# Reordering the opening of a fused state-space and gated-FFN kernel: factors read from PSUM, an earlier cast, and a new order of loads, masks and filler matmuls

## The chip, the cores and the metric

The kernel runs on one core of one Trainium2 chip. The metric is the device time of one execution in microseconds (us); lower is better. A core has five engines that work side by side and wait for each other by semaphores: TensorE (PE in the profile, with its weight loads shown apart as PEld), VectorE (DVE), ScalarE (ACT), GpSimd (POOL) and SyncE (SP), which only starts transfers here.

## The reference, cut to what matters

Two stages follow each other. The first is a chunked scan for 4 batches of 8 heads, 768 tokens, head size 32 and state size 16. With `cum` the cumulative sum of `log a` in a chunk:

```python
M = einsum('bhin,bhjn->bhij', Cc, Bc) * exp(cum[i] - cum[j]) * causal
y = einsum('bhij,bhjd->bhid', M, xc) + einsum('bhin,bhnd->bhid', Cc, state) * exp(cum)
state = exp(sum(la)) * state + sum_j(Bc * xc * exp(cum[-1] - cum))
```

The second takes the 3,072 x 256 result as tokens of a gated feed-forward net with 1,536 hidden units:

```python
out = (maximum(x @ w_gate, 0) * (x @ w_val)) @ w_out
```

## The kernel before, in words

The kernel works in pairs of 128-token chunks (256 tokens, "pair p"; three pairs make a batch, twelve make the whole) and in blocks of 512 tokens for the feed-forward net. Decays are not taken through logarithms: a cumulative product of `a` is scanned, C is multiplied by it and B by its reciprocal, so that `exp(cum[i] - cum[j])` comes out of the product of the two.

A pair goes through these steps, each a helper. `load_bc` and `load_x` bring B, C and x. `scale_wide(p, j, eng)` (line 303) multiplies C (j = 1) or B (j = 0) by the factors in the tile `wfac` and writes bf16. `transp(p, k, apart)` (line 356) transposes the result on PE, and `tevac(p, beng, ceng)` (line 369) brings it from PSUM to SBUF: `BT` by one copy on `beng`, `CT` by a multiplication with a mask on `ceng` (two ScalarE instructions, or one VectorE instruction). `G_wide(p)` (line 411) multiplies CT by BT into four PSUM banks, g0 to g3. `gmask(p, q, eng, psum)` applies the causal mask to bank q, either from PSUM or from a bf16 copy that `gcopy(p, q)` made on ScalarE before. `cast_x(p, eng)` makes x bf16, `adds(p)` forms the new state from B and x, `carry` and `pass_on` scale and hand the state on, `inter_wide(p)` adds the state's share and `D_wide(p, qs)` (line 515) the masked part of the result for the banks `qs`. `yevac_wide(p, A_, V)` evacuates the result of the pair to `yT`, one half on ScalarE, the other on VectorE.

The feed-forward net reads `yT`. `gvh(b, f, u, later)` (line 677) does one slice of 128 hidden units for half a block: four matmuls, then the ReLU on ScalarE at once, and a product on VectorE (`finish`), which `later=True` lets the caller place. Its own first lines show that the ReLU belongs to the call itself:

```python
        r = ffn.tile([128, 512], BF16, tag="r", name="r", bufs=5)[:, 0:256]
        nc.scalar.activation(r, gv_[:, 0], AF.Relu)
```

`factors()` gets the cumulative products of batch 0 into PSUM by matmuls. `scan(0, H)` scans all batches from `a_sb` on VectorE, and `decay()` (line 249) later turns that scan by fp32 matmuls into factors for the other batches, which `decay_factors()` copies to `scaleBC`. `weights(f0, f1)` starts transfers of the gate and value weights from GpSimd's queue. `keep_warm(n)` puts n matmuls on PE whose result nobody reads.

The order is written out by hand: lines 768 to 846 are the opening, one call after the other, and `in_order(tc)` (line 15) ties every engine to the order of the program, so that no instruction overtakes an earlier one on its engine. Across engines only the data and the buffers decide. PSUM tiles named by `bank` share five slots.

Of the kernel before, what the change touches and what calls it, by code (L numbers as in the profile page):

```python
# [29 lines left out]
def kernel(  # L30
# [46 lines left out]
    st = {}  # L77

    def load_bc(p, j, *qs):
        s = st.setdefault(p, {})  # L80
        if "bcr" not in s:
            s["bcr"] = raw.tile([128, NH, 2, 2, N], FP32, tag="bcr", name="bcr")
            if p == 2:
                nc.vector.memset(s["bcr"][0:1, 0, 1, 0, 0:1], 0.0)
        b, s0 = p // PPB, p % PPB * 256
        n = NH // len(qs)
        for i, q in enumerate(qs):
            hs = slice(i * n, (i + 1) * n)
            q.dma_start(
                out=s["bcr"][:, hs, j].rearrange("p h r n -> p h (r n)"),  # L90
                in_=(B, C)[j][b, hs, s0:s0 + 256, :].rearrange(
                    "h (p r) n -> p h (r n)", r=2))

    def load_x(p, *qs):
        xr = raw.tile([128, NH, 2, D], FP32, tag="xr", name="xr")
        if p == 2:
            nc.vector.memset(xr[0:1, 0, 0, 0:1], 0.0)
        b, s0 = p // PPB, p % PPB * 256
        n = NH // len(qs)
        for i, q in enumerate(qs):  # L100
            hs = slice(i * n, (i + 1) * n)
            q.dma_start(out=xr[:, hs].rearrange("p h r d -> p h (r d)"),
                        in_=x[b, hs, s0:s0 + 256, :].rearrange(
                            "h (p r) d -> p h (r d)", r=2))
        st.setdefault(p, {})["xr"] = xr
# [30 lines left out]
    nc.vector.memset(first, 0.0)  # L136
    load_bc(0, 1, nc.sync, nc.scalar)
    load_bc(0, 0, nc.sync, nc.scalar)
    a_sb = glob.tile([2 * BH, H], FP32)
    nc.sync.dma_start(out=a_sb, in_=a.rearrange("b h (w s) -> (b h w) s", w=2))  # L140
    load_x(0, nc.sync, nc.scalar)
    load_bc(1, 1, nc.sync)
    load_bc(1, 0, nc.scalar)
    load_x(1, nc.sync)
# [41 lines left out]
    def keep_warm(n, rhs=warm):  # L186
        w = bank("w", (128, 128))
        for _ in range(n):
            nc.tensor.matmul(out=w, lhsT=warm, rhs=rhs, start=True, stop=True)  # L189
# [5 lines left out]
    def weights(f0, f1, which=(0, 1)):  # L195
        fs = slice(f0 * 128, f1 * 128)
        for j in which:
            w, src = ((wg, moe_w_gate), (wv, moe_w_val))[j]
            nc.gpsimd.dma_start(  # L199
                out=w[:, :, fs], in_=src[:, fs].rearrange("(k p) f -> p k f", k=2))  # L200
# [12 lines left out]
    def factors():  # L213
        d = bank("fac", (128, 2, NH, PPB))
        for r in range(2):
            for i in range(2):
                nc.tensor.matmul(
                    out=d[64 * i:64 * i + 64, r].rearrange("p h k -> p (h k)"),
                    lhsT=cp0[:, r:128:2], rhs=idr[:, i:R:2], start=(r == 0), stop=True,
                    tile_position=(0, 64 * i), skip_group_check=True)  # L220
        return d
# [14 lines left out]
    def scan(s0, s1):  # L236
        nc.vector.tensor_tensor_scan(
            out=cp[:, s0:s1], data0=a_sb[:, s0:s1],
            data1=zero1.to_broadcast([2 * BH, s1 - s0]),
            initial=cp[:, s0 - 1:s0] if s0 else 1.0, op0=ALU.mult, op1=ALU.add)  # L240

    def middle():
        nc.vector.reciprocal(rmid, cp[:, H - 1:H])
        nc.vector.tensor_scalar_mul(pick[:, 0], pairs[:, 0], rmid)
# [3 lines left out]

    def decay():

        bank_ = mm.tile([128, HC * 2 * NB * 8 + 16], FP32, tag="tp", name="dec")
        n = HC * 2 * NB * 8
        d = bank_[:, 0:n].rearrange("p (k w b h) -> p k w b h", k=HC, w=2, b=NB)
        st["dec3"] = d3 = bank_[:, n:n + 16].rearrange("p (r h) -> p r h", r=2)
        for r in range(2):
            for i in range(2):
                nc.tensor.matmul(
                    out=d3[64 * i:64 * i + 64, r], lhsT=cp[:, i * 128 + r:i * 128 + 128:2],
                    rhs=pick[:, 0, NH:2 * NH], start=(r == 0), stop=True,
                    tile_position=(0, 64 * i), skip_group_check=True)  # L260
        for k in range(HC):
            nc.tensor.matmul(  # L262
                out=d[:, k].rearrange("p w b h -> p (w b h)"),
                lhsT=cp[:, k * 128:(k + 1) * 128],
                rhs=pick.rearrange("p w h -> p (w h)"),
                start=False, stop=True, skip_group_check=True)
        st["dec"] = d

    def decay_factors():
        d = st["dec"]  # L270
        nc.scalar.copy(out=fac3[:, 1], in_=st["dec3"])
        for w in range(2):
            cs = slice(w * HC, (w + 1) * HC)
            nc.scalar.copy(
                out=scaleBC[:, :, cs, 1, :].rearrange("p b k h -> p k b h"), in_=d[:, :, w])

    def inverse(b0, b1):
        for b in range(b0, b1):
# [24 lines left out]
    def scale_wide(p, j, eng):  # L303
        s = st[p]
        if p >= FIRST:
            s["bs"] = bs = tok[p % NTOK]
            src = s["bcr"].rearrange("s (t q) j r n -> s j r t q n", t=2)[:, j]
            for t in range(2):
                k = 2 * j * (1 + t)
                eng.tensor_tensor(  # L310
                    out=bs[:, k:k + 2].rearrange("s k (q t n) -> s k t q n", q=4, t=2)[:, :, t],
                    in0=src[:, :, t],
                    in1=fac3[:, j, :, 4 * t:4 * t + 4].to_broadcast([128, 2, 4, N]),
                    op=ALU.mult)
            return
        if "bs" not in s:
            s["bs"] = bs = att.tile([128, 4, 128], BF16, tag="bs", name="bs")
            s["tin"] = [[bs[:, 2 * j + r] for r in range(2)] for j in range(2)]
        src = s["bcr"].rearrange("s (t q) j r n -> s j r t q n", t=2)[:, j]
        f = wfac[:, j, :, :, p]  # L320
        for t in range(2):
            eng.tensor_tensor(  # L322
                out=s["bs"][:, 2 * j:2 * j + 2].rearrange(
                    "s k (q t n) -> s k t q n", q=4, t=2)[:, :, t],
                in0=src[:, :, t],
                in1=f[:, :, 4 * t:4 * t + 4].to_broadcast([128, 2, 4, N]),
                op=ALU.mult)
# [17 lines left out]
    def cast_x(p, ceng):  # L345
        s = st[p]
        cast = ceng.copy if ceng is nc.scalar else ceng.tensor_copy
        xb = att.tile([128, 2 * NH * D], BF16, tag="xb", name="xb")
        if p < NWIDE:
            cast(xb, s["xr"].rearrange("s h r d -> s (h r d)"))  # L350
            s["xb"] = xb.rearrange("s (h r d) -> s h r d", h=NH, r=2)
        else:
            cast(xb, s["xr"].rearrange("s i h d -> s (i h d)"))
            s["x"] = [xb[:, i * NH * D:(i + 1) * NH * D] for i in range(2)]
# [74 lines left out]
    def gmask(p, q, eng, psum=False):  # L429
        s = st[p]  # L430
        d = s["gw"][:, q]
        m = (wmask if p < FIRST else wmask3).unsqueeze(2).to_broadcast([128, 2, 2, 128])
        eng.tensor_tensor(out=d, in0=s["gp"][q] if psum else d, in1=m, op=ALU.mult)  # L433

    def gcopy(p, q):
        s = st[p]
        nc.scalar.copy(out=s["gw"][:, q], in_=s["gp"][q])
# [328 lines left out]
    V, A_, P_ = nc.vector, nc.scalar, nc.gpsimd  # L766

    keep_warm(22)
    d = factors()
    decays(0)  # L770
    keep_warm(8)
    nc.vector.tensor_copy(wfac[:, 1], d)
    nc.vector.memset(wg[0:1, 0, 0:1], 0.0)
    weights(0, 2)
    weights(2, 4)
    weights(4, 6, (0,))
    scale_wide(0, 1, V)
    nc.vector.reciprocal(wfac[:, 0, :, :, 0], wfac[:, 1, :, :, 0])
    scale_wide(0, 0, V)
    transp(0, 1, False)  # L780
    keep_warm(4)
    transp(0, 0, True)
    tevac(0, A_, V)
    nc.vector.reciprocal(wfac[:, 0, :, :, 1:3], wfac[:, 1, :, :, 1:3])
    scan(0, H)
    scale_wide(1, 1, P_)
    scale_wide(1, 0, P_)
    weights(4, 6, (1,))
    keep_warm(6)
    G_wide(0)  # L790
    keep_warm(7)
    gcopy(0, 0)
    gmask(0, 2, V, True)
    keep_warm(5, st[0]["gw"][:, 0, 0, 0])
    cast_x(0, A_)
    decays(1)
    adds(0)
    gmask(0, 3, V, True)
    keep_warm(4, st[0]["gw"][:, 3, 0, 0])
    gmask(0, 0, V)  # L800
    gmask(0, 1, V, True)
    pass_on(0, 0)
    carry(0, 0)
    middle()
    inter_wide(0)
    D_wide(0, (2, 3, 0))
    D_wide(0, (1,))
    turn(1, True)
    keep_warm(2)
    yevac_wide(0, A_, V)  # L810
    load_bc(2, 1, nc.sync)
# [3 lines left out]
    weights(8, NF)  # L815
    weights_out(0, NF // 2)
    weights_out(NF // 2, NF)
    tevac(1, V, A_)
    cast_x(1, V)
    pass_on(0, 1)  # L820
# [1 line left out]
        for f in fs:  # L822
            gvh(b, f, u)

    f0 = gvh(0, 0, 0, True)
    G_wide(1)
    decay()
    adds(1)
# [201 lines left out]
```

## Time and profile before

| What | Value |
|---|---|
| Time, median of 3 runs | 124.46 us (124.38 to 124.65) |
| Span of the profiled execution | 122.7 us |
| PE busy | 118.1 us (96%) |
| VectorE busy | 88.0 us (72%) |
| ScalarE busy | 76.3 us (62%) |
| GpSimd busy | 48.2 us (39%) |
| Granted TensorE clock | 1.0 of full |

The span of the profile is the one traced execution from its first to its last instruction; the time is measured around it and is a little longer. "Busy" is the share of the span in which an engine had at least one instruction running. The page also gives a row of busy tenths in forty slices, and the chain of waits that ended last. In the timeline of an engine each line has a start, a duration, the engine, the line of the kernel, the operation and the tiles that it writes and reads; where several of one kind follow each other they are merged with "x4" and the like. A bracket at the end gives the idle time before the instruction and what ended it.

### The profile page before, as it was taken

Reading aid. Unit: us, or ns where it says so; the run is one execution under the profiler, and the core shown is the slowest. Engines: PE = TensorE matmul, PEld = TensorE weight load, DVE = VectorE, ACT = ScalarE, POOL = GpSimd, SP = SyncE. Lnnn points to the kernel's source line nnn. Section 1 sums busy time; section 2 is a strip of 40 time slices with the busy share of each in tenths; the row PEclk is TensorE's granted clock in tenths of the full one; section 3 lists DMA queues with packets and bytes.
Section 4 is the critical chain, followed back from the end, with each engine's and each line's share of the span. In section 5 each row is a group of like instructions: output and inputs, shape, how many; then the busy total and the mean of one; then the engine's idle time right before and its main releaser. Section 6 shows DMA issues by size and latency. Waiting matters only on the chain.

```text
span 122.7 us, 3665 instructions
## 1 busy us (share of the span) xinstructions
PE 118.1 (96%) x1404; PEld 82.4 (67%) x1404; DVE 88.0 (72%) x200; ACT 76.3 (62%) x169; POOL 48.2 (39%) x108
## 2 busy tenths in 40 slices
PE   6989999999999999999999999999999999999990
PEld 6856784577875478874577864677854678844790
DVE  4798988872799864988763897855987656788410
ACT  0467688835987725786635886545877447876420
POOL 6499989361455127360351806033600033000000
DMA  3999999996979995999999498960580002200022
GB/s 63 220 208 146 171 192 194 189 172 103 115 89 139 143 142 143 103 150 205 150 114 140 154 136 138 110 117 0 189 52 0 0 0 91 85 0 0 0 91 86
DMA packets 77489, 13.93 MB, mean 113 GB/s; under 512 B 70064, under 2 KB 77472, under 8 KB 77472
## 3 DMA queue, kind: packets, MB, share of 16 engines
q1 hardware_dynamic: 70128, 10.61, 54.2%
q0 software_dynamic: 4288, 2.36, 14.1%
q10 hardware_dynamic: 3056, 0.72, 2.7%
q8 instruction: 11, 0.18, 0.6%
q14 instruction: 6, 0.05, 0.1%
HBM read 11.13 MB, written 3.15 MB: 116 GB/s over the span
## 4 chain that ended last, share of the span: by engine, by line
PE 92%; POOL 4%; DVE 1%; issue 1%; DVEq 0%
PE o L713 26%; PE gv L686 21%; PE gate L668 15%; PE val L671 15%; PE y L643 2%; PE g L548 2%; PE w L189 2%; POOL wg L199 2%; POOL bs L322 1%; PE y L632 1%; PE o L707 1%; PE A_ps L601 1%; PE g L418 1%; POOL wv L199 1%; PE y L523 1%; PE dec L262 1%
## 5 line engine op out<-in xcount | busy, mean ns | idle before, releaser
L675 DVE TENSOR_TENSOR h<-r,val 128x512 bf16<-128x512 bf16 x44 | 30.0, 685 | 7.3 <-ACT r L674 7.2
L713 PE MATMUL o<-wo,h 128*128 128x256 bf16 x276 | 33.1, 273 | 0.0
L674 ACT ACTIVATE r<-gate 128x512 bf16<-128x512 f32 x44 | 26.3, 597 | 9.7 <-PE gate L668 9.3
L713 PEld LDWEIGHTS <-h 128*128 128x128 bf16 x276 | 25.9, 98 | 5.3 <-issue 1.7
L668 PE MATMUL gate<-yT,wg 128*128 128x512 bf16 x88 | 26.2, 379 | 0.0
L671 PE MATMUL val<-yT,wv 128*128 128x512 bf16 x88 | 26.2, 379 | 0.0
L692 DVE TENSOR_TENSOR h<-r,gv 128x256 bf16<-128x256 bf16 x56 | 22.5, 419 | 2.6 <-ACT r L689 1.8
L689 ACT ACTIVATE r<-gv 128x256 bf16<-128x256 f32 x56 | 21.2, 386 | 2.3 <-PE gv L686 0.2
L686 PE MATMUL gv<-yT,wg 128*128 128x256 bf16 x112 | 21.5, 273 | 0.0
L686 PE MATMUL gv<-yT,wv 128*128 128x256 bf16 x112 | 21.4, 273 | 0.0
L556 POOL TENSOR_SCALAR_AFFINE_SELECT gs<-gs 128x512 bf16<-128x512 bf16 (+1 forms) x16 | 8.0, 523 | 30.0 <-ACT gs L567 30.0
L573 DVE TENSOR_TENSOR gs<-g,maskUT 128x512 bf16<-128x512 f32 x16 | 10.3, 685 | 11.4 <-issue 5.6
L338 POOL TENSOR_TENSOR tok<-bcr,scaleBC 128x128 bf16<-128x128 f32 x32 | 12.2, 409 | 14.1 <-DMA bcr<-in_B_dram 13.0
L671 PEld LDWEIGHTS <-wv 128*128 128x128 bf16 x88 | 8.6, 98 | 10.4
L668 PEld LDWEIGHTS <-wg 128*128 128x128 bf16 x88 | 8.6, 98 | 8.9
L686 PEld LDWEIGHTS <-wv 128*128 128x128 bf16 x112 | 11.0, 98 | 1.3
L686 PEld LDWEIGHTS <-wg 128*128 128x128 bf16 x112 | 10.2, 98 | 1.9 <-DVE yT L536 0.2
L567 ACT CAST gs<-g 128x512 bf16<-128x512 f32 x8 | 4.7, 589 | 6.7 <-PE g L548 6.7
L656 ACT CAST yT<-y 128x512 bf16<-128x512 f32 x8 | 4.7, 586 | 5.1 <-PE y L643 2.5
L433 DVE TENSOR_TENSOR gs<-g,wmask 128x512 bf16<-128x512 f32 x9 | 5.9, 680 | 2.6 <-PE g L418 2.6
L189 PE MATMUL w<-warm 128*128 128x128 bf16 x49 | 5.5, 284 | 1.1 <-DVE tmask L163 1.1
L189 PEld LDWEIGHTS <-warm 128*128 128x128 bf16 x58 | 5.0, 126 | 1.7 <-DVE tmask L163 1.1
(122 smaller groups left out, 115.8 us busy)
## 6 DMA issues: line engine op xcount, KB each, us to landing
xr<-in_x_dram SPq DMA_DIRECT2D x17, 128.0 KB, 3.2
out_dram<-ob SPq DMA_DIRECT2D x3, 512.0 KB, 3.2
bcr<-in_C_dram SPq DMA_DIRECT2D x17, 64.0 KB, 2.9
bcr<-in_B_dram SPq DMA_DIRECT2D x17, 64.0 KB, 2.9
out_dram<-ob SPq DMA_DIRECT2D x4, 256.0 KB, 3.5
xr<-in_x_dram SPq DMA_DIRECT2D x3, 256.0 KB, 4.1
wo<-in_moe_w_out_dram POOLq DMA_DIRECT2D x2, 384.0 KB, 8.5
wg<-in_moe_w_gate_dram POOLq DMA_DIRECT2D x4, 128.0 KB, 4.0
```

The costliest lines, as they stand in the source:

```text
L189: nc.tensor.matmul(out=w, lhsT=warm, rhs=rhs, start=True, stop=True)
L338: eng.tensor_tensor(out=dst[:, t, j * (1 + t)], in0=src[:, j, :, t], in1=f[:, j, :, 4 * t:4 * t + 4].to_broadcast([128, 2, 4, N]), op=ALU. ...
L556: nc.gpsimd.affine_select(out=dst, in_=dst, pattern=[[0, n], [1, 128]], compare_op=ALU.is_ge, fill=0.0, base=0, channel_multiplier=-1)
L573: nc.vector.tensor_tensor(out=d[:, q], in0=g[q], in1=m, op=ALU.mult)
L668: nc.tensor.matmul(out=g, lhsT=wg[:, k, fs], rhs=yT[:, k, tk], start=(k == 0), stop=(k == 1))
L671: nc.tensor.matmul(out=v, lhsT=wv[:, k, fs], rhs=yT[:, k, tk], start=(k == 0), stop=(k == 1))
L674: nc.scalar.activation(r, g, AF.Relu)
L675: nc.vector.tensor_tensor(out=fst[b][:, f], in0=r, in1=v, op=ALU.mult)
L686: nc.tensor.matmul(out=gv_[:, j], lhsT=w[:, k, fs], rhs=yT[:, k, tk], start=(k == 0), stop=(k == 1), skip_group_check=True)
L689: nc.scalar.activation(r, gv_[:, 0], AF.Relu)
L692: nc.vector.tensor_tensor(out=fst[b][:, f, u * 256:(u + 1) * 256], in0=r, in1=gv_[:, 1], op=ALU.mult)
L713: nc.tensor.matmul(out=o[:, ts % 2], lhsT=fst[b][:, f, ts * 128:(ts + 1) * 128], rhs=wo[:, f], start=(f == 0), stop=(f == NF - 1), skip_gr ...
```

## The change

All edits lie in the first 13 us, but for the shape of the matmuls in `decay()`. They aim at getting pair 0 through its steps sooner and at letting the weights and the first feed-forward slice come earlier.

1. x of pair 0 is loaded ahead of `a_sb` on SyncE's queue.
2. The factors of pair 0 are read where they lie: C is scaled by the PSUM tile `fac` itself, the reciprocal for B of pairs 0 and 1 is taken from it in one instruction, and the copy into `wfac` goes to ScalarE. The reciprocal for pair 2 moves behind `middle()`.
3. The six first weight transfers are started before anything is scaled; the sixth no longer waits behind GpSimd's scaling of pair 1.
4. x of pair 0 is cast before `G_wide(0)`, `adds(0)` comes before the masks, bank 1 also gets a ScalarE copy, and the masks go 2, 0, 1, 3, so `D_wide` leaves bank 3 for last. The counts of filler matmuls change.
5. The first feed-forward slice `f0` and `transp(1, 0)` now stand in front of `tevac(1)`, in that order; before, `f0` stood behind `tevac(1)`, `cast_x(1)` and `pass_on(0, 1)`.
6. `decay()` leaves out batch 0, whose factors nobody reads: 48 moving columns in place of 64.

```diff
-    a_sb = glob.tile([2 * BH, H], FP32)
-    nc.sync.dma_start(out=a_sb, in_=a.rearrange("b h (w s) -> (b h w) s", w=2))
     load_x(0, nc.sync, nc.scalar)
+    a_sb = glob.tile([2 * BH, H], FP32)
+    nc.sync.dma_start(out=a_sb, in_=a.rearrange("b h (w s) -> (b h w) s", w=2))
...
-                lhsT=cp[:, k * 128:(k + 1) * 128],
-                rhs=pick.rearrange("p w h -> p (w h)"),
+                lhsT=cp[:, k * 128:(k + 1) * 128], rhs=pick[:, :, NH:],
...
-        f = wfac[:, j, :, :, p]
+        f = fac[:, :, :, 0] if p == 0 and j else wfac[:, j, :, :, p]
...
     keep_warm(22)
-    d = factors()
+    fac = factors()
+    nc.vector.memset(wg[0:1, 0, 0:1], 0.0)
+    for f in (0, 2, 4):
+        weights(f, f + 2)
     decays(0)
-    keep_warm(8)
-    nc.vector.tensor_copy(wfac[:, 1], d)
-    nc.vector.memset(wg[0:1, 0, 0:1], 0.0)
-    weights(0, 2)
-    weights(2, 4)
-    weights(4, 6, (0,))
+    keep_warm(6)
     scale_wide(0, 1, V)
-    nc.vector.reciprocal(wfac[:, 0, :, :, 0], wfac[:, 1, :, :, 0])
+    nc.vector.reciprocal(wfac[:, 0, :, :, 0:2], fac[:, :, :, 0:2])
+    nc.scalar.copy(out=wfac[:, 1], in_=fac)
     scale_wide(0, 0, V)
...
     tevac(0, A_, V)
-    nc.vector.reciprocal(wfac[:, 0, :, :, 1:3], wfac[:, 1, :, :, 1:3])
     scan(0, H)
+    cast_x(0, A_)
     scale_wide(1, 1, P_)
     scale_wide(1, 0, P_)
-    weights(4, 6, (1,))
-    keep_warm(6)
+    keep_warm(4)
     G_wide(0)
     keep_warm(7)
+    adds(0)
     gcopy(0, 0)
     gmask(0, 2, V, True)
     keep_warm(5, st[0]["gw"][:, 0, 0, 0])
-    cast_x(0, A_)
+    gcopy(0, 1)
+    gmask(0, 0, V)
     decays(1)
-    adds(0)
+    keep_warm(4, st[0]["gw"][:, 2, 0, 0])
+    gmask(0, 1, V)
+    keep_warm(4, st[0]["gw"][:, 1, 0, 0])
     gmask(0, 3, V, True)
-    keep_warm(4, st[0]["gw"][:, 3, 0, 0])
-    gmask(0, 0, V)
-    gmask(0, 1, V, True)
     pass_on(0, 0)
     carry(0, 0)
     middle()
+    nc.vector.reciprocal(wfac[:, 0, :, :, 2], wfac[:, 1, :, :, 2])
     inter_wide(0)
-    D_wide(0, (2, 3, 0))
-    D_wide(0, (1,))
-    turn(1, True)
+    D_wide(0, (2, 0, 1))
+    D_wide(0, (3,))
+    transp(1, 1, True)
     keep_warm(2)
     yevac_wide(0, A_, V)
...
     weights_out(NF // 2, NF)
+    f0 = gvh(0, 0, 0, True)
+    transp(1, 0, True)
     tevac(1, V, A_)
     cast_x(1, V)
     pass_on(0, 1)
...
-    f0 = gvh(0, 0, 0, True)
     G_wide(1)
     decay()
```

More of the change, by code (lines that the diff above doesn't have):

```diff
@@ L138 @@
     load_bc(0, 0, nc.sync, nc.scalar)
+    load_x(0, nc.sync, nc.scalar)
     a_sb = glob.tile([2 * BH, H], FP32)
     nc.sync.dma_start(out=a_sb, in_=a.rearrange("b h (w s) -> (b h w) s", w=2))
-    load_x(0, nc.sync, nc.scalar)
     load_bc(1, 1, nc.sync)
@@ L249, in decay @@
     def decay():
[L251 to L254, printed above, removed]
+        n = HC * 2 * (NB - 1) * NH
+        bank_ = mm.tile([128, n + 2 * NH], FP32, tag="tp", name="dec")
+        d = bank_[:, 0:n].rearrange("p (k w b h) -> p k w b h", k=HC, w=2, b=NB - 1)
+        st["dec3"] = d3 = bank_[:, n:].rearrange("p (r h) -> p r h", r=2)
         for r in range(2):
@@ L262, in decay @@
             nc.tensor.matmul(
-                out=d[:, k].rearrange("p w b h -> p (w b h)"),
-                lhsT=cp[:, k * 128:(k + 1) * 128],
-                rhs=pick.rearrange("p w h -> p (w h)"),
+                out=d[:, k].rearrange("p w b h -> p w (b h)"),
+                lhsT=cp[:, k * 128:(k + 1) * 128], rhs=pick[:, :, NH:],
                 start=False, stop=True, skip_group_check=True)
@@ L274, in decay_factors @@
             nc.scalar.copy(
-                out=scaleBC[:, :, cs, 1, :].rearrange("p b k h -> p k b h"), in_=d[:, :, w])
+                out=scaleBC[:, 1:, cs, 1, :].rearrange("p b k h -> p k b h"), in_=d[:, :, w])
     def inverse(b0, b1):
```

## The prediction, made before the changed kernel was run

> **What bounds the kernel now.** I first read the page, then the engines' busy time from the first feed-forward matmul to the last one, then the chain of waits through the opening, then the timelines of ScalarE and VectorE there.
>
> ```profile
> span 122.7 us, 3665 instructions
> PE 118.1 (96%) x1404; PEld 82.4 (67%) x1404; DVE 88.0 (72%) x200; ACT 76.3 (62%) x169; POOL 48.2 (39%) x108
> ```
>
> ```profile
> 10.30:119.70 109.40, 109.40 (x1260) 75.58 (x1260) 79.89 (x168) 72.36 (x160) 40.55 (x88) 1.00 0.70 109
> ```
>
> The second line (stretch, its length, then busy PE, PEld, DVE, ACT, POOL) says that PE is never idle between 10.30 and 119.70 us. The end is therefore set by when PE's unbroken run begins and by how much work is in it. Only two things can move the time: a shift of that beginning, or work taken out of the run.
>
> ```profile
> 7.80 0.72 POOL wg L199
> 8.52 0.01 issue
> 8.54 1.70 POOL bs L322 x4
> 10.24 0.05 issue
> 10.28 0.28 PE tpb L367 x2
> 10.57 0.11 PE w L189 x2
> 10.68 0.45 PE gv L686 x4
> 11.13 0.39 PE g L418 x16
> 11.51 0.34 PE dec L257 x8
> 11.85 0.81 PE dec L262 x6
> ```
>
> This chain (start, us, what) is a near tie, not GpSimd's alone: the run begins with transp(1,0), which waited for GpSimd's scaling of pair 1, but f0's matmuls (gv) also need pair 0's result, and that is ready at 10.38, as the VectorE lines below show. The thing to see is what stands between f0 and G_wide(1): nothing. f0 fills PE for 0.45 us just while pair 1's transposes are evacuated.
>
> ```profile
> 9.92 0.37 ACT L540 CAST yT<-y 128x256 bf16<-128x256 f32 x1 [0.91 <-PE Aps L523]
> 10.19 0.84 ACT L385 ACTIVATE CT<-tp,tmask 128x256 bf16<-128x256 bf16 x2
> 10.92 0.35 ACT L486 ACTIVATE Sw<-T,dec 128x64 bf16<-128x64 f32 x1
> 11.16 0.38 ACT L689 ACTIVATE r<-gv 128x256 bf16<-128x256 f32 x1
> ```
>
> ```profile
> 6.39 0.89 DVE L237 TENSOR_TENSOR_SCAN cp<-a_sb,zero 64x384 f32<-64x384 f32 x1
> 7.21 1.25 DVE L433 TENSOR_TENSOR gs<-g,wmask 128x512 bf16<-128x512 f32 x2
> 8.38 0.47 DVE L433 TENSOR_TENSOR gs<-gs,wmask 128x512 bf16<-128x512 bf16 x1
> 8.78 0.68 DVE L433 TENSOR_TENSOR gs<-g,wmask 128x512 bf16<-128x512 f32 x1
> 9.38 0.14 DVE L243 RECIPROCAL rmid<-cp 64x1 f32<-64x1 f32 x1
> 9.56 0.34 DVE L244 TENSOR_SCALAR pick<-identf,rmid 64x32 f32<-64x32 f32 x1
> 9.96 0.42 DVE L540 CAST yT<-Aps 128x256 bf16<-128x256 f32 x1
> 10.61 0.29 DVE L392 COPY BT<-tpb 128x256 bf16<-128x256 bf16 x1
> ```
>
> On ScalarE the two CT multiplications of pair 1 stand ahead of f0's ReLU (r) and end at 11.03; G starts at 11.09. BT ended at 10.90. So G waits for CT, and CT follows the evacuation of pair 0 without a gap.
>
> **What the Trainium skill says.** "TensorE: Matmul & The Clock Gate", Part 1, says that ScalarE and VectorE take instructions strictly in order. The trace agrees: every timeline above follows the program, so an instruction that waits holds up all behind it. "DMA: Bandwidth & Descriptors", Queues, rings and completion order, says that descriptors of a ring are consumed in ring order and that a DMA engine takes turns between rings packet by packet. No run here shows the swap, but SyncE's `a_sb` (issued 2.29, 3.4 us to landing) does land before the x behind it (2.90, 3.9 us). "VectorE: DVE Perf Modes", The perf-mode tier table, gives a bf16 tensor_tensor from SBUF twice the rate of one from PSUM; here 128x512 take 0.41 to 0.47 us against 0.68 us. The TensorE page, Why this matters for your kernels, warns of idle gaps over some 3 us; the gap that I find below is under 1 us, and the gaps of this trace (clock 1.00) cost nothing visible.
>
> **Part by part: pair 0.** Scaling C from PSUM starts at 4.19 instead of 4.43: the copy's 0.24 us is gone from VectorE. The operand from PSUM isn't in the trace for this shape: at best the 0.286 us of one such scaling stays, at worst it grows by some 0.1 us; I take it unchanged, because the tier table named above has fp32 tensor_tensor at the single rate from either memory. The reciprocal over 32 columns costs 0.34 instead of 0.25, so 0.1 comes back. CT of pair 0 therefore starts at 5.38 instead of 5.53, and G(0) 0.15 earlier. The copy into wfac on ScalarE (0.2 us, from about 4.46, after its table load) lies beside VectorE's scaling. Six filler matmuls in place of eight end before C is scaled; they are no cost.
>
> The reciprocal at 6.13 (0.26 to the next start) leaves this place, so scan could start at 5.98. But `a_sb` is now behind half of x: issued at about 2.90, and its bytes moved to behind 512 short packets. In before the SyncE queue's packet count stands in `a_sb` from about 3.9 to 5.05 us, and the landing came 0.65 later. 512 short packets at the 150 per 0.25 us that this queue made beside ScalarE's take 0.85 us. So it lands between 6.0 (the rest goes faster) and 6.8 (the earlier weights compete); I take 6.45. Scan then starts at 6.45 and gains nothing; behind it on VectorE wait all four masks and the rest of pair 0, so the first mask starts at 7.27 (scan to mask was 0.82) instead of 7.21. ScalarE's cast of x (0.62) now stands at about 6.15, so its copies of g0 and g1 start near 6.74 and 7.22 and are done before VectorE needs them. The masks go at starts of 7.27, 7.84, 8.24 and 8.64 (0.57 behind a PSUM mask, 0.40 behind a bf16 one), and the last ends at 9.32 instead of 9.46: one mask became bf16 and saves 0.19. Bank 3's eight D matmuls then end at about 9.75. On VectorE middle() and the third reciprocal (0.25) come first: 9.24, 9.42, 9.72, evacuation 9.93 to 10.35. Before it was 9.96 to 10.38. Pair 0 thus gains only 0.03 us where the scan is late, and 0.25 where it isn't: f0 starts at 10.1 to 10.4, say 10.40.
>
> **Weights.** The flag (memset) moves from 4.34 to about 3.3, the first start from 4.73 to about 3.65. One start at 0.93 and five at 0.72 end at 8.2; the four scalings (1.70) end at 9.9 instead of 10.24. That removes the GpSimd wait from transp(1,0), but f0 at 10.40 is later, so it is worth nothing by itself. Weights for f0 land with a second to spare.
>
> **f0 ahead of transp(1,0) and tevac(1).** This sets the result. On PE f0 (0.45) now stands in front of the transposes: they start at 10.85, BT's copy comes 0.33 later as before, G 0.48 after that: 11.65. On ScalarE f0's ReLU now stands in front of CT. Behind the waiting ReLU are queued both CT multiplications and the state's scaling; G and through it all of PE wait for CT. The ReLU starts about 0.42 after f0's first matmul (two of 0.11, then the drain and a semaphore; L668 to L674 shows 0.63 with matmuls twice as long), at 10.82. The next ScalarE start follows after 0.30 (three ReLUs took 0.96). CT takes 0.84: 11.96. G starts at 12.0 instead of 11.09. Its gap on PE, from about 11.1 to 12.0, has no filler in it, since f0 was that filler: +0.9.
>
> **decay().** Six fp32 records of 64 columns take 0.81 us, 135 ns each. If columns set it, 48 save a quarter, 0.20; if the loading of 128 weight columns (0.74 us busy for the six) sets it, nothing. I take 0.10. This is inside PE's run, so it counts in full. The smaller copies on ScalarE are beside other work.
>
> Sum: +0.91 - 0.10 = +0.8 us. All work behind G keeps its order and its distances, so nothing makes it up: 124.46 + 0.8 = 125.26.
>
> **The rivals.**
> A, `a_sb` later still: if weights and x push the landing to 6.8 or more, or a filler matmul or PSUM slot stops PE, scan and masks shift by another 0.4 to 0.7, and the time is near 125.8. For it: the DMA row of the page is full from 2.5 to 10 us. Against: the first weight packets started only 2.4 us after their issue, so about 6.05.
> B, the head gains in full: scan at 5.98, f0 at 10.1, decay saves 0.2. CT still ends at 11.66: +0.6 - 0.2, 124.86. For it: the transfer's bytes are few.
> C, faster: GpSimd's branch is the only bound, G's operands don't wait for the ReLU, and the run begins 0.4 earlier: 124.06. For it: the chain names GpSimd for 1.7 us up to 10.24. Against: CT at 11.03 already was G's last operand, and the ReLU is now in front of it.
> D, gains and the new gap cancel: f0 would have to start at 9.6 or so; 124.46.
>
> **How the numbers follow.** Forecast 0.53, A 0.18, B 0.15, C 0.08, D 0.06. The range 124.75 to 126.0 takes in the forecast, B and A and leaves C and D out, and some of A's tail. Faster 0.08; within 0.2% (0.25 us) 0.08, which is D and the lower edge of B; slower 0.84.
>
> **What would show it.** In the changed profile ScalarE's r (L689) stands before CT of pair 1 and after an idle time; PE is idle 0.7 to 1.0 us ahead of g; that g starts between 11.6 and 12.5. The scan starts near 6.45 if `a_sb` holds it, near 6.0 if not. The L262 group shows 0.6 to 0.8 us. After g PE is unbroken. I am wrong if CT comes ahead of r, if f0 starts before 9.7, or if PE has idle time after g that the kernel before lacked.

## The result, and the profile after

The changed kernel takes 130.96 us (median of 4, 130.36 to 131.87) where the kernel before takes 124.45 (124.38 to 124.65) beside it: a ratio of 1.053, 95% interval 1.045 to 1.060. The forecast was 125.26 with 126.0 as its upper end. The direction was right; of a loss of 6.5 us the forecast had 0.8. Executions of one and the same kernel can differ by several us, mostly because the TensorE clock is halved in some of them and for different lengths of time, so ranges are given, and ratios leave out executions over 1.5% above the fastest of their kernel. The profiled execution of the changed kernel is the one of 131.87 us, so its parts add up to 7.5 us rather than 6.5.

The page of the changed kernel; the last row is the granted clock in forty slices of 3.3 us:

```profile
span 130.2 us, 3661 instructions
PE 122.9 (94%) x1398; PEld 85.2 (65%) x1404; DVE 88.6 (68%) x199; ACT 77.3 (59%) x171; POOL 48.0 (37%) x108
...
PEclk9995555999999999999999999999999999999999
```

The span is 7.5 us longer, yet PE is busy only 4.8 us longer, with less work. The clock row has fives: from about 10 to 23 us the clock was halved, which the profile of before doesn't show. The busy times by stretch (stretch, length, then busy PE, PEld, DVE, ACT, POOL, and the granted clock) of the changed kernel and then of the kernel before:

```profile
6.00:9.60 3.60, 2.65 (x54) 1.62 (x52) 2.46 (x4) 2.27 (x6) 3.60 (x8) 1.00 1.38 213
9.60:23.10 13.50, 11.60 (x169) 7.84 (x170) 7.44 (x22) 5.32 (x15) 5.38 (x9) 0.50 1.29 166
```

```profile
6.00:9.60 3.60, 3.18 (x92) 2.12 (x91) 3.56 (x9) 2.05 (x6) 3.58 (x7) 1.00 1.40 206
9.60:23.10 13.50, 13.34 (x181) 9.14 (x179) 11.68 (x31) 11.08 (x31) 12.70 (x27) 1.00 1.26 176
```

PE was busy 0.53 us less between 6.0 and 9.6, where it stood idle for 0.95 us in all; then the clock is 0.50 for 13.5 us. Where PE waited, the timeline of PE in the changed kernel says (brackets: idle time before, and what ended it):

```profile
8.84 0.38 PE L230 MATMUL dec<-ends,heads 48*128 48x6 f32 x2 [0.79 <-DVE gs L432]
...
10.40 0.60 PE L189 MATMUL w<-gs,warm 128*128 128x128 bf16 x4 [0.84 <-DVE gs L432]
...
12.61 0.59 PE L685 MATMUL gv<-yT,wg 128*128 128x256 bf16 x2
...
14.82 0.65 PE L417 MATMUL g<-CT,BT 32*64 32x256 bf16 x16 [0.99 <-ACT CT L384]
```

Three idle times, each under 1 us: two behind VectorE's masks, one behind CT. Only the first (8.05 to 8.84) lies wholly ahead of the fall of the clock; the second had just begun (9.56), and the third came 4 us later, when each matmul was slow already. The timeline of VectorE gives the cause of the first two:

```profile
5.43 0.68 DVE L387 TENSOR_TENSOR CT<-tp,tmask 128x512 bf16<-128x512 bf16 x1
7.26 0.95 DVE L237 TENSOR_TENSOR_SCAN cp<-a_sb,zero 64x384 f32<-64x384 f32 x1 [1.14 <-DMA a_sb<-in_a_dram]
8.13 0.66 DVE L432 TENSOR_TENSOR gs<-g,wmask 128x512 bf16<-128x512 f32 x1
8.71 1.62 DVE L432 TENSOR_TENSOR gs<-gs,wmask 128x512 bf16<-128x512 bf16 x2
10.26 0.68 DVE L432 TENSOR_TENSOR gs<-g,wmask 128x512 bf16<-128x512 f32 x1
```

The scan waited 1.14 us for `a_sb`, and two bf16 masks took 1.62 us instead of 0.8. ScalarE shows the third, the ReLU waiting and CT behind it:

```profile
13.66 0.38 ACT L688 ACTIVATE r<-gv 128x256 bf16<-128x256 f32 x1 [1.28 <-PE gv L685]
13.94 0.83 ACT L384 ACTIVATE CT<-tp,tmask 128x256 bf16<-128x256 bf16 x2
```

One sum orders all that follows: the start of `G_wide(1)`, and the rest of the span behind it. All columns but the last two are starts, in us.

| Kernel | scan | last mask | f0 | G | rest behind G | span |
|---|---|---|---|---|---|---|
| before | 6.39 | 8.78 | 10.53 | 11.09 | 111.61 | 122.7 |
| forecast | 6.45 | 8.64 | 10.40 | 12.0 | 111.5 | 123.5 |
| after | 7.26 | 10.26 | 12.61 | 14.82 | 115.38 | 130.2 |

So 3.73 of the 7.5 us lie ahead of G and 3.77 behind it. The forecast's row is its own starts, with 0.10 taken from the rest. For f0 of before the table takes PE's timeline (10.53); the chain printed ahead of the prediction gives 10.68.

The 3.77 behind G are the halved clock, as one and the same matmul further on shows, first in before, then in the changed kernel:

```profile
16.19 0.38 PE L686 MATMUL gv<-yT,wg 128*128 128x256 bf16 x2
```

```profile
23.61 0.38 PE L685 MATMUL gv<-yT,wg 128*128 128x256 bf16 x2
```

It stands 5.10 us behind G before and 8.79 us behind it now. So 3.69 of the 3.77 have arisen by the time at which the clock is back, and in between PE waits for nothing longer than 0.2 us.

### The profile page after: what moved, and what is told of

The parts are those of the page before. It is cut to its first block, busy times and chain, and to the rows that moved or that the text cites. A ratio compares the mean times of both kernels' runs of the same rounds, so it can differ in the third digit from the quotient of the medians.

```text
span 130.2 us, 3661 instructions
## 1 busy us (share of the span) xinstructions
PE 122.9 (94%) x1398; PEld 85.2 (65%) x1404; DVE 88.6 (68%) x199; ACT 77.3 (59%) x171; POOL 48.0 (37%) x108
## 3 DMA queue, kind: packets, MB, share of 16 engines
q0 software_dynamic: 4288, 2.36, 13.6%
## 4 chain that ended last, share of the span: by engine, by line
PE 93%; DVE 2%; ACT 1%; issue 1%; DVEq 0%
PE o L712 24%; PE gv L685 22%; PE val L670 15%; PE gate L667 14%; PE w L189 4%; PE y L642 2%; PE g L547 2%; DVE gs L432 2%; PE g L417 1%; PE y L522 1%; PE y L631 1%; PE dec L262 1%; PE o L706 1%; PE A_ps L600 1%; ACT CT L384 1%
## 5 line engine op out<-in xcount | busy, mean ns | idle before, releaser
L712 PEld LDWEIGHTS <-h 128*128 128x128 bf16 x276 | 25.9, 98 | 5.3 <-issue 1.7
L667 PE MATMUL gate<-yT,wg 128*128 128x512 bf16 x82 | 24.9, 379 | 0.0
L685 PE MATMUL gv<-yT,wg 128*128 128x256 bf16 x112 | 23.1, 289 | 0.1
L685 PE MATMUL gv<-yT,wv 128*128 128x256 bf16 x112 | 22.9, 288 | 0.0
L337 POOL TENSOR_TENSOR tok<-bcr,scaleBC 128x128 bf16<-128x128 f32 x32 | 12.2, 407 | 13.2 <-DMA bcr<-in_B_dram 12.1
L670 PEld LDWEIGHTS <-wv 128*128 128x128 bf16 x88 | 8.6, 98 | 10.4
L667 PEld LDWEIGHTS <-wg 128*128 128x128 bf16 x88 | 8.6, 98 | 8.9
L685 PEld LDWEIGHTS <-wv 128*128 128x128 bf16 x112 | 11.6, 103 | 1.9
L685 PEld LDWEIGHTS <-wg 128*128 128x128 bf16 x112 | 10.7, 102 | 2.8 <-issue 0.6
L432 DVE TENSOR_TENSOR gs<-g,wmask 128x512 bf16<-128x512 f32 x8 | 5.3, 682 | 3.3 <-PE g L417 3.3
## 6 DMA issues: line engine op xcount, KB each, us to landing
xr<-in_x_dram SPq DMA_DIRECT2D x17, 128.0 KB, 3.2
wg<-in_moe_w_gate_dram POOLq DMA_DIRECT2D x4, 128.0 KB, 4.7
```

Of the source, the lines that this page charges most:

```text
L337: eng.tensor_tensor(out=dst[:, t, j * (1 + t)], in0=src[:, j, :, t], in1=f[:, j, :, 4 * t:4 * t + 4].to_broadcast([128, 2, 4, N]), op=ALU. ...
L667: nc.tensor.matmul(out=g, lhsT=wg[:, k, fs], rhs=yT[:, k, tk], start=(k == 0), stop=(k == 1))
L670: nc.tensor.matmul(out=v, lhsT=wv[:, k, fs], rhs=yT[:, k, tk], start=(k == 0), stop=(k == 1))
L685: nc.tensor.matmul(out=gv_[:, j], lhsT=w[:, k, fs], rhs=yT[:, k, tk], start=(k == 0), stop=(k == 1), skip_group_check=True)
L712: nc.tensor.matmul(out=o[:, ts % 2], lhsT=fst[b][:, f, ts * 128:(ts + 1) * 128], rhs=wo[:, f], start=(f == 0), stop=(f == NF - 1), skip_gr ...
```

## The experiments

Each is compared with the kernel before on the same chip: 1 to 4 ran on one, 5 to 8 on a second, 9 to 14 on a third. G is the start of `G_wide(1)` in the profiled execution, and the rest is span less G.

**1. `a_sb` first again** (the changed kernel without edit 1).

```diff
-    load_x(0, nc.sync, nc.scalar)
     a_sb = glob.tile([2 * BH, H], FP32)
     nc.sync.dma_start(out=a_sb, in_=a.rearrange("b h (w s) -> (b h w) s", w=2))
+    load_x(0, nc.sync, nc.scalar)
```

> The changed kernel with a_sb loaded ahead of x again. If the late landing of a_sb (7.2 us) is what starts it all, the scan starts near 6.0 us, the bf16 masks end before or beside the start of GpSimd's scaling, PE's idle stretches between 8 and 10.4 us shrink to under 0.4 us each, the clock stays at 1.00 and the time falls to 125.0 to 125.8 us (what is left is the later G of pair 1). If the gap behind f0 or the fewer fillers halve the clock by themselves, it stays above 129 us with a clock near 0.95.

Measured: 129.41 us (128.0 to 129.52), 1.034 (1.027 to 1.041). Scan at 5.99, so `a_sb` was what held it. But mask 0 then stood idle for 1.10 us behind PE's filler matmuls and started at 9.02; G 14.47, rest 113.13, with PE slow up to about 13.5 and again from 16.6 to 20.2. A late scan is one cause, not the only one.

**2. Fillers in the idle times, first try** (the changed kernel with 46 filler matmuls).

```diff
     gmask(0, 0, V)
+    keep_warm(14)
     decays(1)
...
+    keep_warm(18)
     keep_warm(4, st[0]["gw"][:, 1, 0, 0])
...
     transp(1, 0, True)
+    keep_warm(14)
```

> The changed kernel with 46 more filler matmuls that wait for nothing, in the three idle stretches of PE (14 ahead of decays(1), 18 ahead of the fillers that wait for mask 1, 14 behind transp(1,0)). If the halved clock is most of the loss, the clock stays at 1.00, a_sb still lands at 7.2 and G of pair 1 starts near 13.5 us, and the time is 126.3 to 127.3 us. If the clock is a side effect and waiting is the loss, the time stays at 130 to 131 us.

Measured: 131.97 us (130.74 to 132.55), 1.057 (1.049 to 1.064). PE was still slow when they came (a 128x128 filler took 311 ns instead of 219), so they overran and pushed G to 15.21. Behind G the clock was full, and yet the rest is 114.49. PE waited there for data, once for longer than 2 us:

```profile
37.70 0.42 PE L417 MATMUL g<-turned 32*64 32x256 bf16 x16 [2.47 <-DMA turned<-tok]
```

This transfer waits for GpSimd, which runs on without a pause from pair 2's B, for which it had waited 2.01 us (24.45), to the scaling of pair 3. So the number expected was missed, and the run shows a second way to lose time: pair 2's B came late. That load was issued at 13.73 here (before: 10.85), behind all the weight transfers that now start earlier, and took 10.6 us; before no load of B or C took over 5.2 us.

**3. Masks 0 and 1 from PSUM** (the changed kernel).

```diff
-    gmask(0, 0, V)
+    gmask(0, 0, V, True)
...
-    gmask(0, 1, V)
+    gmask(0, 1, V, True)
```

> The changed kernel with masks 0 and 1 read from PSUM (the ScalarE copies stay, unused but as the fillers' flag). If VectorE's two-input mask from SBUF was stopped by GpSimd's scaling (1.29 us for one that takes 0.41 to 0.47), no mask takes over 0.70 us, the last of the four ends near 10.5 instead of 10.94 us, and the time falls by 0.3 to 0.5 us if the clock still halves, to about 126 us if the shorter idle time keeps the clock. If the mask was slow for another reason (its ScalarE copy, a slot), mask 0 stays over 1 us.

Measured: 132.16 us (130.72 to 132.21), 1.057 (1.050 to 1.063). No mask was long any more (three in 1.89 us), but the first of the three waited 0.88 us for fillers, as in 1, and PE was slow all the same, from the start to 23.5 us: the 128x256 matmuls took 417 ns (median) instead of 273, though the clock record says 1.00 throughout (rest 115.25). The stretched mask isn't the root of the lost clock.

In the opening of 1, 2 and 3 the clock didn't fall behind a gap: it came up late. Every profile here starts slow, with 128x128 fillers of some 312 ns. In before and in the changed kernel they take 221 from 6.5 us on, in 1, 2 and 3 still 305 to 314 at 8, although PE had stood idle for only 0.04 us between 4.5 and 6.4. So idle time is no likely reason there; what kept it slow stays open.

**4. f0 and transp(1,0) ahead of tevac(1), alone** (edit 5 on the kernel before), **and 6. the same with 16 fillers behind them** (the `keep_warm` line, in 6 only).

```diff
-    turn(1, True)
+    transp(1, 1, True)
...
+    f0 = gvh(0, 0, 0, True)
+    transp(1, 0, True)
+    keep_warm(16)
     tevac(1, V, A_)
...
-    f0 = gvh(0, 0, 0, True)
     G_wide(1)
```

> The kernel before with edit 5 alone: f0 and transp(1,0) in front of tevac(1). The forecast's step: ScalarE's ReLU of f0 goes ahead of CT of pair 1, G of pair 1 starts 0.9 us later (12.0 for 11.09), the clock stays 1.00, and the time is 125.2 to 125.5 us. If CT does not wait for the ReLU, the time stays within 0.2 us of 124.45. If a gap of 0.9 us on PE halves the clock, it is 128 us or more.

> The kernel before with edit 5 alone, as in e4_f0_move, and 16 fillers that wait for nothing behind transp(1,0), in PE's idle 1.1 us. In e4 three executions took 125.6 us and four took 127.6 to 129.5. If the idle time of PE is what halves its clock in the latter, every execution here takes 125.4 to 125.8 us. If something else makes them slow, the spread from 125.6 to 129.5 stays.

Measured for 4: 1.007 (1.004 to 1.011); three executions at 125.61 to 125.67, four at 127.64 to 129.51, whose recorded mean clock is 0.973 or 0.986; where in the span it fell was not traced. For 6: 1.008 (1.006 to 1.011), all eleven at 125.62 to 126.91. PE's timeline in 4 and then in 6:

```profile
10.53 0.38 PE L686 MATMUL gv<-yT,wg 128*128 128x256 bf16 x2 [0.30 <-DVE bcr L84]
...
12.33 0.42 PE L418 MATMUL g<-CT,BT 32*64 32x256 bf16 x16 [1.09 <-ACT CT L385]
```

```profile
10.51 0.38 PE L686 MATMUL gv<-yT,wg 128*128 128x256 bf16 x2 [0.30 <-DVE bcr L84]
...
11.05 1.06 PE L189 MATMUL w<-warm 128*128 128x128 bf16 x16
12.30 0.42 PE L418 MATMUL g<-CT,BT 32*64 32x256 bf16 x16 [0.20 <-ACT CT L385]
```

G is later by 1.24 and 1.21, and both profiles show full clock and the rest of 111.67 and 111.6. The wait itself costs the same; with work in the gap that nobody reads, the executions with a halved clock are gone. One gap of some 1.1 us came with them in 4 of 7. Experiments 4 and 6 ran on different chips, but before was alike on both: one of 10 executions above 126 beside 4 (126.45), one of 52 beside 6 (126.49).

**5. `a_sb` behind x, alone** (edit 1 on the kernel before).

```diff
-    a_sb = glob.tile([2 * BH, H], FP32)
-    nc.sync.dma_start(out=a_sb, in_=a.rearrange("b h (w s) -> (b h w) s", w=2))
     load_x(0, nc.sync, nc.scalar)
+    a_sb = glob.tile([2 * BH, H], FP32)
+    nc.sync.dma_start(out=a_sb, in_=a.rearrange("b h (w s) -> (b h w) s", w=2))
```

> The kernel before with edit 1 alone: x of pair 0 loaded ahead of a_sb. If the order on SyncE's queue by itself makes a_sb land near 7.0 us, the scan starts 0.6 to 0.8 us later than before (6.39) and the time is 125.0 to 125.4 us at a full clock. If the early weights were needed for that, a_sb lands by 6.5 and the time stays within 0.3 us of 124.5.

Measured: 1.005 (1.003 to 1.008); 13 of 22 executions at 125.06 to 125.93, the others at 126.93 to 128.65. VectorE's timeline:

```profile
7.36 0.95 DVE L237 TENSOR_TENSOR_SCAN cp<-a_sb,zero 64x384 f32<-64x384 f32 x1 [0.88 <-DMA a_sb<-in_a_dram]
```

The scan is 0.97 later than before without any earlier weight transfer. The order on the queue is enough.

**7. The changed kernel without edits 1 and 5, 8. edit 4 alone on the kernel before, and 9. kernel 7 with masks 0 and 1 from PSUM** (as in 3).

> The changed kernel without edits 1 and 5 (a_sb ahead of x, f0 and the transposes of pair 1 placed as before). If these two are the whole loss, G of pair 1 starts near 11 us and the time is 124.2 to 124.8 us. If the new order of casts, masks and fillers (edit 4) loses time by itself, because mask 0 may only overwrite gw0 when the five fillers that read it are done and because GpSimd's scaling meets the masks from SBUF, G of pair 1 is past 12 us and the time is 125.5 us or more, with part of PE's work at half clock.

> The kernel before with edit 4 alone (x cast and adds(0) ahead, bank 1 copied too, masks in the order 2, 0, 1, 3, D with bank 3 last, the new fillers). If edit 4 is neutral or a gain where a_sb is in time, the last mask ends at 9.3 to 9.5 us and the time is 124.2 to 124.7 us. If x is late for the cast that now stands in front of the copies of g (it landed at 6.8 us in the kernel before), the copies start near 7.4, mask 0 waits for them and the fillers, the last mask ends near 10.2 us and the time is 125.0 us or more.

> As e7_no_swap_no_move, with masks 0 and 1 read from PSUM. In e7 the two masks from SBUF took 2.00 us together beside GpSimd's scaling (8.17 to 9.71). If GpSimd and VectorE exclude each other where both read two tensors from SBUF, the masks here follow at 0.57 us each whatever GpSimd does, the last of the four ends by 10.2 us instead of 10.94, PE's idle stretch of 1.52 us shrinks below 0.9 and the time of the undisturbed executions falls to about 124.8 us. If they were slow for another reason, mask 0 stays near 1 us.

Measured: 7: 1.005 (1.000 to 1.009) over its four fastest executions (up to 126.42), but 14 of 18 at 127.3 to 130.1; profile G 13.02, rest 115.38. 8: 1.008 (1.004 to 1.011), 5 of 12 executions at 126.9 to 129.6; profile G 12.14, rest 111.66. 9: 128.75 us (128.01 to 130.11), 1.029 (1.024 to 1.035); G 12.94, rest 113.36. VectorE in 7:

```profile
6.89 0.69 DVE L432 TENSOR_TENSOR gs<-g,wmask 128x512 bf16<-128x512 f32 x1
8.34 2.00 DVE L432 TENSOR_TENSOR gs<-gs,wmask 128x512 bf16<-128x512 bf16 x2 [0.76 <-PE w L189]
```

Here the scan was in time, and still the masks are late twice over. First, mask 0 is done in place, in the very bf16 copy that five fillers read (`keep_warm(5, st[0]["gw"][:, 0, 0, 0])`); with mask 0 moved to second place it must wait until PE has run them. This wait is in 1, 3, 7, 8 and 9 (0.51 to 1.10 us). Second, the masks are stretched beside GpSimd's scaling; from PSUM (9) the same stretch holds three in 1.89. In 9 that brought the last mask's end forward from 10.94 to 10.33 but G by only 0.08, and the time expected of it was missed. PE was slow from about 9.8 to 13.3, just ahead of G and behind it; later, at full speed, it waited 0.9 us for the transpose of pair 3, the way seen in 2 (pair 2's B took 10.2 us here).

**10. Edits 2, 3 and 6 on the kernel before, 12. edit 3 alone, 14. kernel 12 with mask 0 from PSUM** (the `gmask` lines, in 14 only).

```diff
     d = factors()
+    nc.vector.memset(wg[0:1, 0, 0:1], 0.0)
+    for f in (0, 2, 4):
+        weights(f, f + 2)
...
-    weights(4, 6, (1,))
...
-    gmask(0, 0, V)
+    gmask(0, 0, V, True)
```

> The kernel before with edits 2, 3 and 6 alone: factors from PSUM, all six weight transfers first, 48 columns in decay; loads, masks, fillers and f0 as before. If these parts give what the forecast's sums say (0.15 to 0.4 us on pair 0, GpSimd's scaling ended at 9.9 instead of 10.24, 0.1 in decay), G of pair 1 starts at 10.6 to 10.9 and the time is 123.9 to 124.3 us. If the early weights slow the loads of B, C and x, a_sb or C lands later, the masks meet GpSimd's scaling, and the time is 124.6 us or more.

> The kernel before with edit 3 alone: the six weight transfers started first. If the weights' early packets hold up a_sb, it lands at 6.3 us or later instead of 5.7, the scan starts later than 6.39 and the time is 124.8 us or more. If they do not, the scan stays at 6.4, GpSimd's scaling ends 0.3 us earlier and the time is 124.2 to 124.5 us.

> As e12_weights_only, with mask 0 read from PSUM. In e12 the mask from SBUF started at 8.39 us, 0.3 behind GpSimd's scaling, and took 1.53 us. If it is the two engines' access to SBUF, the mask takes 0.68 us here, no execution takes more than 125.5 us and the median is 124.4 to 124.8 us. If the early weights disturb the loads, executions of 126.8 to 130.8 us remain.

In 10 the reciprocal for pair 2 stands behind `cast_x(1, V)` instead of `middle()`.

Measured: 10: 0.9975 (0.9955 to 0.9996), G 10.79, rest 111.61; but 5 of 20 executions at 126.4 to 129.1. 12: 0.999 (0.997 to 1.001), 8 of 20 at 126.8 to 130.8. 14: 1.004 (1.002 to 1.007), 21 of 22 at 124.62 to 126.51 and one at 128.24. The timelines of VectorE and then GpSimd around mask 0 in 12, then VectorE in 14 and in 10:

```profile
8.39 1.53 DVE L433 TENSOR_TENSOR gs<-gs,wmask 128x512 bf16<-128x512 bf16 x1
```

```profile
8.09 1.54 POOL L322 TENSOR_TENSOR bs<-bcr,wfac 128x128 bf16<-128x128 f32 x4
```

```profile
7.21 2.45 DVE L433 TENSOR_TENSOR gs<-g,wmask 128x512 bf16<-128x512 f32 x4
```

```profile
8.11 0.41 DVE L432 TENSOR_TENSOR gs<-gs,wmask 128x512 bf16<-128x512 bf16 x1
```

In 12 mask 0 was issued 0.30 us after GpSimd began and ended 0.29 after GpSimd's end: 1.53 us. In 10 it was issued at 8.11, GpSimd at 8.22, and it took 0.41. From PSUM (14) four masks go at their usual pitch straight through GpSimd's work. This is what the Trainium skill's "SBUF — State Buffer", Who interferes with whom, says: a VectorE instruction with two SBUF inputs contends with a GpSimd instruction that reads SBUF, and whichever was issued first has the shared ports for the whole of that instruction while the other blocks. The trace agrees here, and in 7 and the changed kernel, where VectorE lost as in 12. But in 1, 2, 5 and 8 a bf16 mask was also issued after GpSimd's first scaling and took only 0.43 to 0.71 us, while GpSimd's four took 1.72 to 1.94 us instead of 1.51. The ports can change hands between GpSimd's four instructions; what decides it, no run shows. The page was not among those the prediction used.

In the profiled execution of 12 (129.90 us) the clock fell later, from 25.9 to 29.3 us. Ahead of it PE waited for pair 2's B once more:

```profile
24.07 0.78 POOL L322 TENSOR_TENSOR bs<-bcr,wfac 128x128 bf16<-128x128 f32 x2 [2.37 <-DMA bcr<-in_B_dram]
```

```profile
24.91 0.28 PE L367 MATMUL tp<-ident,bs 128*128 128x128 bf16 x2 [2.60 <-POOL bs L322]
```

Its stretched mask held pair 0 up by 1.07 us (f0 at 11.60), so that load was issued at 11.91 instead of 10.85, and it took 12.1 us. In 14 it was issued at 11.05 and took 6.9. That fits 14's fewer long executions, whose cause would then be the late load and not the mask as such; the executions without a trace can't tell.

**11. Fillers again, sized to the waits** (the changed kernel).

```diff
-    keep_warm(6)
+    keep_warm(8)
     scale_wide(0, 1, V)
...
-    keep_warm(4)
+    keep_warm(6)
     G_wide(0)
...
     gmask(0, 0, V)
+    keep_warm(7)
     decays(1)
...
+    keep_warm(9)
     keep_warm(4, st[0]["gw"][:, 1, 0, 0])
...
     transp(1, 0, True)
+    keep_warm(14)
```

> The changed kernel with fewer and better placed extra fillers than e2_fill (4 more ahead of G of pair 0, 7 ahead of decays(1), 9 ahead of those that wait for mask 1, 14 behind transp(1,0)). If the halved clock makes some 4 us of the loss, some executions keep or regain the clock early and take 126.5 to 128 us. If the direct waits are the larger part, all stay at 129.5 us or more.

Measured: 126.85 us (four executions, 126.80 to 126.91), 1.016 (1.012 to 1.020) against 1.053 (1.045 to 1.060) without them. Its page and PE's timeline:

```profile
span 125.1 us, 3735 instructions
...
PEclk9999999999999999999999999999999999999999
```

```profile
12.21 0.94 PE L189 MATMUL w<-warm 128*128 128x128 bf16 x14
13.47 0.42 PE L417 MATMUL g<-CT,BT 32*64 32x256 bf16 x16 [0.31 <-ACT CT L384]
```

No five in the clock row; the rest behind G is 111.63, the 111.61 of before. The 34 added matmuls compute nothing that is read, and the kernel with them is 4.1 us faster. Four of them stand ahead of `G_wide(0)`, where edit 4 had taken four out; what these do and what those in the idle times do wasn't separated.

**13. Kernel 10 with mask 0 ahead of mask 3** (and the fillers on mask 2's copy).

```diff
-    keep_warm(5, st[0]["gw"][:, 0, 0, 0])
+    keep_warm(5, st[0]["gw"][:, 2, 0, 0])
+    gmask(0, 0, V)
     cast_x(0, A_)
...
-    gmask(0, 0, V)
```

> As e10_edits_2_3_6, with the mask from SBUF second in the order (2, 0, 3, 1) and the five fillers waiting for mask 2 in place of the copy of g0, so that it runs near 7.5 us, before GpSimd's scaling of pair 1 starts at 8.2. If a scaling that starts first is what stops that mask in some executions, none takes more than 125.3 us, and the median is 124.0 to 124.3 us. If the spread of e10 (5 of 20 above 126.4 us) has another cause, it stays.

Measured: 1.002 (1.000 to 1.004), 3 of 22 executions at 126.9 to 129.2, the others at 124.29 to 125.83; G 11.46. Mask 0 was unstretched (7.95, 0.41), but the version is no gain. And since the long executions that it was meant to end are still there, a stretched mask is not what makes them.

## Why the prediction failed, by its own steps

**f0 ahead of tevac(1): mechanism right, size short.** The ReLU stands in front of CT and G waits for CT, as forecast. Experiment 4 puts G 1.24 later, not 0.9, with f0 where it was: 10.53 in both timelines. The forecast's own sum, 10.40 for f0 and 12.0 for G, is 0.33 short of 4's 12.33. Of that 0.13 is f0's start, which follows the end of the evacuation by 0.15 us (10.38 to 10.53), where the forecast took 0.02 to 0.05. The other 0.2 is the ReLU's start: 0.63 behind f0's first matmul (10.53 to 11.16), where the forecast scaled a measured 0.63 down to 0.42.

**`a_sb`: mechanism right, size short.** Forecast landing and scan at 6.45; measured 7.26, 7.36 (5) and 6.87 (11). These starts are beyond the 6.8 that the forecast gave as its later bound and rival A's beginning. Experiment 5 shows the order alone does it, not the earlier weights. The row of the changed kernel's DMA issues (what, queue, count, KB, us from issue to landing):

```profile
a_sb<-in_a_dram SPq DMA_DIRECT2D x1, 96.0 KB, 4.3
```

Before it was 3.4; issued at 2.97 instead of 2.29, it lands 1.6 us later.

**The masks "at starts of 7.27, 7.84, 8.24 and 8.64": this step failed.** Shifted to the measured first start of 8.13 they would be 8.13, 8.70, 9.10, 9.50; the last began at 10.26. The 0.40 behind a bf16 mask was taken from a place where no GpSimd instruction stood in its way. Earlier weights brought GpSimd's scaling forward to 8.17, as forecast, and just there mask 0 came to stand. So edit 3 was not free: it took nothing from PE but put a longer instruction on VectorE. The wait for the five fillers, which the forecast didn't look for, is hidden here only because the scan is later still; without the swap (1, 7) it takes its place.

**"All work behind G keeps its order and its distances": this is the step that set the error.** The rest behind G is 111.61, 111.67, 111.60, 111.66, 111.61 and 111.63 in before and experiments 4, 6, 8, 10 and 11, all at full clock, and 111.84 and 111.91 in 13 and 14. In the changed kernel it is 115.38. What failed is the price of PE's idle time. The forecast counted a gap under 1 us at its own length and put its effect on the clock at nothing, a reading taken from a trace whose opening is kept full by fillers. Here the clock is halved from 9.65 to 23.3, with one gap of 0.79 us, or 0.95 us of idle time in 3.6, ahead of it. That is 3.77 us behind G, and part of the 3.73 ahead of it (f0 to G took 2.21 instead of the 1.80 of 4). Experiment 11 points the same way: the same order of the work, fillers in the gaps, full clock, the rest of before, 4.1 us less. These 4.1 are not the clock alone: in 11's profile `a_sb` landed about 0.4 earlier, its masks started before GpSimd, and pair 2's B landed 3.4 us earlier (20.2 instead of 23.5). With a full clock in the changed kernel PE might have had to wait for that B, as it did in 2; so filling the gaps and getting the load out early may both be needed.

The sentence fails a second time, where the clock is full: the order of the work behind G holds, but its loads don't keep their times. With four or five of the later weight transfers started ahead of it, the slowest load of B or C took 8.2 to 12.1 us (the changed kernel, 1, 2, 3, 7, 9, 12); with one it took 4.6 to 6.9 (before, 4, 6, 10). That the weights hold it up is the likely reading; no run moved the weights behind it to show it.

**What the skill said of it.** "TensorE: Matmul & The Clock Gate", Part 1, ties the half clock to an idle window of some 3.4 us, and the forecast leaned on that. Its section A second HAM failure mode: psum-queue depth-cycling does tell of a clock that falls under frequent short idle times. The traces here side with the second: from 6 us on, no idle time of PE in the changed kernel's opening is longer than 1 us, and only one of 0.79 us had passed when the clock fell.

**decay(): the lower bound was true.** The instruction group's median is 272 ns for 64 and for 48 columns; six in sequence took 0.88 us in 4 and 0.86 in 10, both at full clock. Not columns but something common to both sets it; their weight loads are 188 ns in both. It saves at most 0.02, not 0.10.

**Weights and the reading from PSUM: right.** GpSimd's sixth start ended at 8.2 and its scaling at 9.7 (forecast 9.9). In 10, without edits 1, 4 and 5, the scan starts at 5.99 and G 0.30 earlier: edits 2, 3 and 6 do gain what the forecast gave pair 0 (0.25), when nothing stands in front.

**Open.** The clock falls behind idle PE time in the changed kernel's profile, and with fillers it stays up in 6 and 11. But in 1, 2 and 3 it was low before any gap, so idle time isn't the only thing that decides; whether the fewer fillers ahead of `G_wide(0)` have a part in that, no run tests. Which share of the idle time is needed is not shown, nor what sets how long the clock then stays down: executions of 4, 5, 7, 10 and 12 differ among themselves. The skill's Part 1 calls the watching window free-running, which would give such a scatter; no run here tests that. Long executions can also come from the wait for pair 2's B, as in 2 and 12, and which of the two it was in those without a trace stays open. Kernel 10 has the lowest ratio of all, but its five long executions of 20 make it no safe gain.

## What to carry to other kernels

When a change puts a wait on TensorE in a stretch that was kept full by fillers, price it twice: the wait itself, and the granted clock after it; then put fillers into the new gap, or keep the work there that hid it. A duration measured beside idle engines holds only beside idle engines: before moving GpSimd work, look which VectorE instruction with two SBUF operands it will now precede. When transfers are started earlier, look which later load now stands behind them. And before moving an in-place instruction forward, look who still reads its operand, filler matmuls included.

## What the runs showed of the hardware

- A single idle time of TensorE of 0.79 us (0.95 us in the 3.6 us up to 9.6) was followed by a halved clock for 13.6 us in the changed kernel. One gap of 1.09 us (4) came with a lower mean clock, 0.973 or 0.986, in four of seven executions; with 16 fillers in it (6) none of eleven had one.
- A bf16 mask of 128x512 from two SBUF tiles took 0.41 us free and 1.53 us when GpSimd's scaling was issued 0.30 us earlier (12). In 1, 2, 5 and 8 it took 0.43 to 0.71 beside GpSimd, and GpSimd's four scalings 1.72 to 1.94 instead of 1.51. From PSUM it showed no change (14).
- The clock record doesn't show everything: in experiment 1 its row is full at 4 to 6 us, yet a 128x128 filler took 312 ns against 219 at full clock; every profile opens so; in experiment 3 it says 1.00 throughout, yet 128x256 matmuls took 417 ns instead of 273 up to 23.5 us. Durations of one known matmul are the surer sign.
- 96 KB issued 0.7 us later, behind half of x on the same queue, landed 1.6 us later (5.7 to 7.3). A load of B took 12.1 us in 12, with five of the later weight transfers started ahead of it on another queue, against 5.2 at most in before.
